# Where one rounding stands in ScalarE's queue, and which engines mask the scores of chunks 4 to 7

## The chip, the core and the metric

The kernel runs on one core of a Trainium2 chip. The core has a matrix engine (TensorE, PE in the profile), a vector engine (VectorE, DVE), a scalar engine (ScalarE, ACT), a general engine (GpSimd, POOL) and a queue that here issues the transfers (SyncE, SP). They run side by side and wait for each other through semaphores. The metric is device time in microseconds (us) of one execution.

## The reference

A gated linear attention (a recurrence over 768 steps for each of 4 batches and 8 heads), followed by two matrix products with a SiLU between them. Inputs: q, k, v, alpha of shape (4, 8, 768, 48), w_in (384, 2048), w_out (2048, 384).

```python
for t in range(S):                                  # S = 768
    state = alpha[:, :, t, :, None] * state + np.einsum('bhd,bhe->bhde', k[:, :, t], v[:, :, t])
    y[:, :, t] = np.einsum('bhd,bhde->bhe', q[:, :, t], state)
x = y.transpose(0, 2, 1, 3).reshape(3072, 384)      # tokens x (heads * 48)
h = x @ w_in
out = (h * (1.0 / (1.0 + np.exp(-h)))) @ w_out
```

## The kernel before

The sequence is cut into chunks of 128 tokens; with 4 batches there are 24 chunks, numbered n = 0 to 23. Each chunk goes through four stages: `products` (transposes of alpha, k, q; running products of alpha by a scan), `scores` (q times k, masked so that a token sees only earlier ones), `values` (masked scores times v, plus the state from before), `states` (the new state). At each step of the main loop the four stages work on neighbouring chunks, and after each stage `fill` puts in other work: at first conversions of weights, later the feed-forward products.

The weights come as 64-bit numbers and are made 32-bit numbers piece by piece. Here is that generator; `rounding` is ScalarE's part, the three `dve` lines are VectorE's. The rounding of the next piece is issued ahead, as soon as the present one's VectorE part is in the queue.

```python
def weights(which):
    # ... pieces: 12 of w_in (128 x 512) for which == 0, 16 of w_out (128 x 384) for which == 1
    def rounding(bits):
        n = bits.shape[1]
        up = upp.tile([128, 512], I32, name="up")[:, 0:n]
        tc.keep_in_program_order(
            act.activation(up, bits.bitcast(U32)[:, :, 0], AF.Copy, scale=2.0**-29))
        return up

    ahead = []
    for i, (dst, src) in enumerate(pieces):
        # ...
        bits = coming.pop(0)                       # a piece that was fetched before
        up = ahead.pop() if ahead else rounding(bits)
        hi, w = bits[:, :, 1], dst.bitcast(I32)
        tc.keep_in_program_order(                  # L623, L624, L625 in the profile
            dve.tensor_scalar(w, hi, 3, 0x3FFFFFFF, ALU.logical_shift_left, ALU.bitwise_and))
        dve.scalar_tensor_tensor(w, hi, -(1 << 30), w, ALU.bitwise_and, ALU.bitwise_or)
        dve.tensor_tensor(w, w, up, ALU.add)
        if i + 1 < len(pieces):
            ahead.append(rounding(coming[0]))      # L609
        fetch()                                    # issues the load of a later piece
        yield
```

The scores. GB is 4, NA is 8: chunks 0 to 3 are masked by a ScalarE copy out of PSUM and a GpSimd select, chunks 4 and up by a VectorE product with a mask.

```python
def scores(n):
    # ... ps: two PSUM banks of the three in ps_attn(); matmuls of kp and qp into them (L757)
    g = c["g"] = work.tile([128, 2, NP, C], F32, name="g")
    for u in range(2):
        if n < GB:
            act.copy(g[:, u], ps[u])                                        # L763
            gps.affine_select(g[:, u], g[:, u], pattern=[[0, NP], [1, C]], compare_op=ALU.is_ge,
                              fill=0.0, base=0, channel_multiplier=-1)      # L764
            continue
        m = mask[:, :, None, :] if n >= NA else mask[:, 0:1, None, :]
        dve.tensor_tensor(g[:, u].rearrange("p (o j) c -> p o j c", o=2),   # L768
                          ps[u].rearrange("p (o j) c -> p o j c", o=2),
                          m.to_broadcast([128, 2, NP // 2, C]), ALU.mult)
    if ci < NCH - 1:
        ps_k = ps_attn()
        # ... transposes of kp into ps_k (L774)
        act.copy(c["kn"], ps_k)                                             # L776
    # ... for ci > 0: the old state is scaled by ScalarE (L780)
```

Other lines that the profile names. L694: transposes of alpha (an), k (kn) and q (qn) on PE; L696: ScalarE's copy of the transposed alpha (al); L699, L728: the two scans on VectorE; L709, L733: its products that make kp and qp; L800: the matmuls of `values`; L805: ScalarE's copy of their result (xt); L815 and L821, L823: the states; L858: the matmuls with w_in (two blocks of 128 columns at a time, six matmuls); L861: SiLU; L971: a VectorE sum of two SiLU results; L980: matmuls with w_out; L498: the loads of weight pieces.

The main loop and the placing of the conversions (SLOTS is 4; marks[0] is 10; a "slot" is one stage's place in a step). `convert(0, k)` runs the generator of w_in until k pieces are done.

```python
def fill(step, slot):
    at = step * SLOTS + slot
    if at < marks[0]:
        if step >= 1:
            convert(0, (at - SLOTS) * 3 // (marks[0] - SLOTS) + 1)
        return
    # ... feed-forward pieces with the conversions that they need

for step in range(STEPS):
    # ...
    stages = [[(scores, 1)], [(products, 0)], [(values, 1)], [(states, 1)]]
    if step == 1:
        stages = stages[1::-1] + stages[2:]        # products of chunk 1, then scores of chunk 0
    # ... for each slot: its stages, then fill(step, slot)
```

So in step 1 the first slot is `products` of chunk 1, followed by the first conversion, and the second slot is `scores` of chunk 0.

Of the kernel before, what the change touches and what calls it, by code (L numbers as in the profile page):

```python
# [355 lines left out]
def quotients(  # L356
# [32 lines left out]
    GB = 4  # L389
# [28 lines left out]
    def ps_attn(n=C):  # L418
        return ps_a.tile([128, 512], F32, name="ps_a").rearrange("p (j c) -> p j c", c=n)
# [18 lines left out]
    NA = 2 * GB  # L438
# [53 lines left out]
    def fetch():  # L492

        if wide and sources:
            src = sources.pop(0)
            n = src.shape[1]
            bits = raw.tile([128, 512, 2], I32, name="bits")[:, 0:n, :]
            nc.sync.dma_start(bits.rearrange("p n w -> p (n w)"), src.bitcast(I32))  # L498
            coming.append(bits)
# [30 lines left out]
    mask = consts.tile([128, 2, C], F32, name="mask")  # L530
    gps.memset(mask, 1.0)
    for odd in range(2):
        for e in range(2):
            m = mask[CH * e : CH * e + CH, odd, :]
# [59 lines left out]
    def weights(which):  # L594

        pieces = [
            (w_in[:, t, c : c + 512], moe_w_in[t * 128 : t * 128 + 128, c : c + 512])  # L600
            for t, c in pieces_in
        ] if which == 0 else [
            (w_out[:, f, :], moe_w_out[f * 128 : f * 128 + 128, :]) for f in range(NFT)]
# [10 lines that stand above are left out]
            if not wide:  # L614
                act.dma_start(dst, src)
                yield
                continue
            assert which == 0 or conv_done[0] == n_conv[0]
            bits = coming.pop(0)
            up = ahead.pop() if ahead else rounding(bits)  # L620
            hi, w = bits[:, :, 1], dst.bitcast(I32)
            tc.keep_in_program_order(
                dve.tensor_scalar(w, hi, 3, 0x3FFFFFFF, ALU.logical_shift_left, ALU.bitwise_and))  # L623
# [4 lines that stand above are left out]
            fetch()  # L628
            yield
# [114 lines left out]
    def scores(n):  # L744
        c = ctxs[n]
        ci, b = c["ci"], c["b"]
        ps = c.pop("blank") if n >= NA else [ps_attn() for _ in range(2)]

        for j in (0, 2, 1, 3):
            for e in range(2 if n >= NA else 1):
                for u in range(2):
                    r = slice(64 * u, 64 * u + D)
                    at = slice(CH * e, CH * e + CH) if n >= NA else slice(0, C)
                    t = slice(CH * (e ^ j // 2) if n >= NA else 0, C)
                    pe.matmul(ps[u][at, j, t], lhsT=c["kp"][r, j, at], rhs=c["qp"][r, j, t],  # L757
                              start=True, stop=True)
        g = c["g"] = work.tile([128, 2, NP, C], F32, name="g")
        for u in range(2):  # L760
            if n < GB:

                act.copy(g[:, u], ps[u])  # L763
                gps.affine_select(g[:, u], g[:, u], pattern=[[0, NP], [1, C]], compare_op=ALU.is_ge,  # L764
                                  fill=0.0, base=0, channel_multiplier=-1)
                continue
            m = mask[:, :, None, :] if n >= NA else mask[:, 0:1, None, :]
            dve.tensor_tensor(g[:, u].rearrange("p (o j) c -> p o j c", o=2),  # L768
                              ps[u].rearrange("p (o j) c -> p o j c", o=2),
                              m.to_broadcast([128, 2, NP // 2, C]), ALU.mult)  # L770
        if ci < NCH - 1:
            ps_k = ps_attn()
            for j in range(NP):
                pe.transpose(ps_k[:, j, :], c["kp"][:, j, :], ident)  # L774
            c["kn"] = work.tile([128, NP, C], F32, name="kn")
            act.copy(c["kn"], ps_k)  # L776
        if ci > 0:
            s = st[b].rearrange("p j u e -> p j (u e)")
            for j in range(NP):
                act.mul(s[:, j], s[:, j], least[:, n, j : j + 1])  # L780
# [192 lines left out]
    def leave(grp, h):  # L973
# [70 lines left out]
        yield  # L1044

    conv = [weights(0), weights(1)]
    n_conv = (NKT * (DF // 512), NFT)
    conv_done = [0, 0]

    def convert(which, upto):  # L1050
        while conv_done[which] < min(upto, n_conv[which]):
            next(conv[which], None)
            conv_done[which] += 1
# [38 lines left out]
    def go_on():  # L1092

        nonlocal done
        next(pieces[done][0], None)
        done += 1
# [4 lines left out]
    SLOTS = 4  # L1101
# [14 lines left out]
    def fill(step, slot):  # L1116

        at = step * SLOTS + slot
        if at < marks[0]:
            if step >= 1:  # L1120
                convert(0, (at - SLOTS) * 3 // (marks[0] - SLOTS) + 1)
            return
        i = next(i for i, m in enumerate(marks[1:]) if at < m)
        a, b = [work_at[n] for n in ([0] + phases)[i : i + 2]]
        due = a + (b - a) * (at - marks[i] + 1) / (marks[i + 1] - marks[i])
        if at % 2 == 0 and step > 3 * GB + 2:
            next(audits, None)
        while work_at[done + 1] <= due and pieces[done][2] <= bridged:
            convert(0, 3 * (done // 2) + 6)
            convert(1, 3 * (done - 6) // 2)  # L1130
            go_on()

    for step in range(STEPS):
        if step == 1:
            load(NIN)
        stages = [[(scores, 1)], [(products, 0)], [(values, 1)], [(states, 1)]]
        if step == 1:

            stages = stages[1::-1] + stages[2:]
        elif step >= NA:  # L1140
            stages = [[(scores, 1)], [(products, 0)], [(values, 1), (states, 1)], [(quotient, 0), (blank, 0)]]
        for slot, group in enumerate(stages):
            for stage, lag in group:
                n = step - lag
                if not 0 <= n < NT:
                    continue
                stage(n)
                if stage is values:
                    bridged = n + 1
                if stage is states and n + 1 + NIN < NA:  # L1150
                    load(n + 1 + NIN)
                if stage is quotient and n + 1 < NT:
                    load(n + 1)
                if stage is states and n + NV < NT:
                    load_v(n + NV)
            fill(step, slot)
            if step * SLOTS + slot >= NA * SLOTS - 1 and conv_done[1] == NFT and not late:
                settle()
# [85 lines left out]
```

## Time and profile before

| what | value |
|---|---|
| time, median of 3 runs | 563.04 us (562.8 to 563.6) |
| span of the profiled run | 561.6 us |
| PE busy | 543.9 us (97%) |
| PE weight loads busy | 492.6 us (88%) |
| DVE busy | 453.0 us (81%) |
| ACT busy | 205.3 us (37%) |
| POOL busy | 15.1 us (3%) |
| mean granted PE clock | 0.994 |
| DMA moved | 63.81 MB, mean 114 GB/s |

How to read the profile's lines. A group or timeline row has the engine, the line of the kernel, the operation, `out<-in` by the program's names, sizes in partitions x elements, and the number of instructions merged into it (x2). In a timeline the first number is the start in us from the start of the span, the second the duration; brackets at the end hold the idle time of that engine just before, and which instruction or transfer ended it. A row of the table of stretches has the stretch in us, its length, then for each engine the busy time with the number of instructions, and last the granted PE clock, the mean busy share of the 16 DMA engines (over 1 when packets overlap) and GB/s. A row of waits has who waited for whom: us in total, how many times, the longest. Each fp32 matmul shows up as two records, so that six matmuls are x12.

### The profile page before, as it was taken

The numbers are of one execution on the slowest core, as the hardware profiler recorded it, in microseconds if no ns is written. First come the engines' busy times: TensorE is split into PE (matmuls) and PEld (weight loads), VectorE is DVE, ScalarE is ACT, GpSimd is POOL, SyncE is SP. The second block draws the span as 40 slices with busy tenths as digits, with TensorE's granted clock in tenths as the row PEclk, the third lists the DMA queues.
The fourth block names the chain that finished last, engine by engine and source line by source line (L and its number), as shares of the span: only waits on it lengthen the run. The fifth ranks groups of instructions, "written<-read, shape, count | busy, mean of one in ns | idle before, by whom it ended". The sixth has DMA issues, their size and how long they took to land.

```text
span 561.6 us, 12420 instructions
## 1 busy us (share of the span) xinstructions
PE 543.9 (97%) x5074; PEld 492.6 (88%) x5074; DVE 453.0 (81%) x829; ACT 205.3 (37%) x406; POOL 15.1 (3%) x36
## 2 busy tenths in 40 slices
PE   5899999999999999999999999999999999999996
PEld 3688887998999999899989999999998999899995
DVE  5797899966999799986998897899895875857731
ACT  2566543213233342443433443434443342332100
POOL 4211000100000000000000000000000000000000
PEclk9899999999999999999999999999999999999998
DMA  9989971143443333333425544435522123334200
GB/s 206 230 241 223 234 183 34 43 126 100 100 107 89 73 97 87 101 87 85 131 70 160 142 108 134 130 81 153 136 69 81 53 85 118 99 94 125 71 30 26
DMA packets 94417, 63.81 MB, mean 114 GB/s; under 512 B 55312, under 2 KB 86032, under 8 KB 94352
## 3 DMA queue, kind: packets, MB, share of 16 engines
q1 hardware_dynamic: 94352, 62.94, 43.3%
q8 instruction: 41, 0.67, 0.5%
q14 instruction: 24, 0.20, 0.1%
HBM read 58.20 MB, written 4.72 MB: 112 GB/s over the span
## 4 chain that ended last, share of the span: by engine, by line
PE 75%; DVE 14%; DMA 5%; SPq 2%; issue 2%; ACT 1%; POOL 0%; DVEq 0%; ACTq 0%
PE ps_o L980 33%; PE ps_m L882 18%; PE ps_m L858 11%; PE ps_a L800 6%; DMA bits<-in_moe_w_out_dram 3%; PE ps_a L757 3%; DVE seen L663 2%; PE ps_a L774 1%; DVE g L896 1%; DMA bits<-in_moe_w_in_dram 1%; DVE u L699 1%; PE ps_a L815 1%; DVE w_out L625 1%; DVE p L728 1%; SPq L456 1%
## 5 line engine op out<-in xcount | busy, mean ns | idle before, releaser
L980 PE MATMUL ps_o<-w_out,g 128*128 128x192 f32 x768 | 133.6, 328 | 1.1 <-DVE o L994 1.1
L980 PEld LDWEIGHTS ps_o<-w_out,g 128*128 128x128 f32 x768 | 125.5, 190 | 3.9 <-DVE o L994 1.5
L980 PE MATMUL ps_o<-wt,g 128*128 128x192 f32 x576 | 100.0, 327 | 0.0
L980 PEld LDWEIGHTS ps_o<-wt,g 128*128 128x128 f32 x576 | 95.1, 190 | 1.5
L858 PE MATMUL ps_m<-xt,w_in 128*128 128x256 f32 x384 | 88.5, 382 | 1.0 <-ACT xt L805 1.0
L858 PEld LDWEIGHTS ps_m<-xt,w_in 128*128 128x128 f32 x384 | 71.0, 190 | 11.0 <-ACT xt L805 1.4
L882 PE MATMUL ps_m<-xc,w_in 128*128 128x256 f32 x288 | 70.1, 379 | 0.0
L882 PEld LDWEIGHTS ps_m<-xc,w_in 128*128 128x128 f32 x288 | 54.0, 190 | 6.4 <-DVE g L896 0.2
L663 DVE TENSOR_REDUCE seen<-bits 128x1 f32<-128x384 int32 (+2 forms) x65 | 42.4, 689 | 16.8 <-DMA bits<-in_moe_w_out_dram 16.5
L893 ACT ACTIVATE g<-g 128x1024 f32<-128x1024 f32 x32 | 33.1, 1055 | 57.5 <-DVE g L896 57.5
L985 DVE TENSOR_TENSOR g<-g 128x512 f32<-128x512 f32 x72 | 48.5, 686 | 5.6 <-PE ps_o L980 5.6
L882 PE MATMUL ps_m<-xc,wx 128*128 128x256 f32 x192 | 50.1, 383 | 0.0
L888 ACT COPY g<-ps_m 128x512 f32<-128x512 f32 x64 | 36.8, 587 | 36.1 <-PE ps_m L882 36.0
L780 ACT ACTIVATE st<-st,least 128x96 f32<-128x96 f32 x80 | 24.1, 364 | 58.4 <-DVE least L702 58.4
L882 PEld LDWEIGHTS ps_m<-xc,wx 128*128 128x128 f32 x192 | 35.0, 190 | 4.2 <-issue 0.4
L896 DVE TENSOR_TENSOR g<-ps_m,g 128x512 f32<-128x512 f32 x56 | 37.4, 683 | 0.8 <-PE ps_m L882 0.5
L699 DVE TENSOR_TENSOR_SCAN u<-al,one 128x516 f32<-128x516 f32 x24 | 29.1, 1212 | 10.4 <-ACT al L696 10.3
L728 DVE TENSOR_TENSOR_SCAN p<-al,inv 128x516 f32<-128x516 f32 x24 | 29.4, 1226 | 5.2 <-PE ps_a L800 4.9
L861 ACT ACTIVATE g<-ps_m 128x512 f32<-128x512 f32 x32 | 19.0, 595 | 39.2 <-PE ps_m L858 39.0
L800 PE MATMUL ps_a<-g,vn 128*32 128x128 f32 x768 | 28.0, 282 | 3.9 <-POOL g L764 3.9
L800 PEld LDWEIGHTS ps_a<-g,vn 128*32 128x32 f32 x768 | 20.3, 112 | 11.2 <-issue 5.5
L768 DVE TENSOR_TENSOR g<-ps_a,mask 128x512 f32<-128x512 f32 x40 | 25.7, 685 | 4.0 <-PE ps_a L757 3.7
(125 smaller groups left out, 620.7 us busy)
## 6 DMA issues: line engine op xcount, KB each, us to landing
bits<-in_moe_w_in_dram SPq DMA_DIRECT2D x24, 512.0 KB, 4.7
bits<-in_moe_w_out_dram SPq DMA_DIRECT2D x32, 384.0 KB, 3.4
at<-in_alpha_dram SPq DMA_DIRECT2D x64, 96.0 KB, 2.4
kt<-in_k_dram SPq DMA_DIRECT2D x64, 96.0 KB, 2.6
qt<-in_q_dram SPq DMA_DIRECT2D x64, 96.0 KB, 2.5
bits<-in_alpha_dram SPq DMA_DIRECT2D x9, 512.0 KB, 3.8
out_dram<-o SPq DMA_DIRECT2D x48, 96.0 KB, 1.9
an<-in_alpha_dram SPq DMA_DIRECT2D x8, 192.0 KB, 5.1
```

The costliest lines, as they stand in the source:

```text
L663: dve.tensor_reduce(seen[kind][which][:, i : i + 1], x, axis=AX, op=op, apply_absolute_value=True))
L699: dve.tensor_tensor_scan(u[:, end - 1 :: -1], sg[:, end:0:-1], one[:, end:0:-1], 0.0, ALU.mult, ALU.add)
L728: dve.tensor_tensor_scan(p[:, 0:end], sg[:, 0:end], iv[:, 0:end], 0.0, ALU.mult, ALU.add)
L768: dve.tensor_tensor(g[:, u].rearrange("p (o j) c -> p o j c", o=2), ps[u].rearrange("p (o j) c -> p o j c", o=2), m.to_broadcast([128, 2, ...
L800: pe.matmul(py[32 * at : 32 * at + 32, t, :], lhsT=w, rhs=x, start=(i < 4), stop=(i >= len(todo) - 4), skip_group_check=True)
L858: pe.matmul(ps[:, e, :], lhsT=w_in[:, t, (f + e) * 128 : (f + e + 1) * 128], rhs=xt[:, t, :], start=(t == 0), stop=(t == NKT - 1))
L882: pe.matmul(ps[:, e], lhsT=block_w(w)[:, 2 * pair + e], rhs=block_x(grp, x), start=(first and e == 0), stop=(e == 1), skip_group_check=True)
L888: act.copy(to, ps)
L893: act.activation(x, x, AF.Silu)
L896: dve.tensor_tensor(to, a, b, op)
L980: pe.matmul(ps, lhsT=x, rhs=w[:, i], start=(first and i == 0), stop=(i == HF - 1), skip_group_check=True)
L985: dve.tensor_tensor(cells(grp, h, pair, *to), cells(grp, h, pair, *x), cells(grp, h, pair, *y), ALU.subtract)
```

## The change

Two things are changed. The first moves one ScalarE instruction. The generator now stops once, in its first piece, right after the first rounding; the first slot of step 1 runs it only up to there, and the second slot, after the scores of chunk 0, runs the rest of the first piece. The rounding of the second piece, which is issued at the end of the first piece, so comes behind ScalarE's copies of the first scores instead of ahead of them. It is meant to keep those copies from waiting for a weight load. The second widens the path by ScalarE and GpSimd from chunks 0 to 3 to chunks 0 to 7; it is meant to take the mask products of chunks 4 to 7 off VectorE.

```diff
@@ weights
             bits = coming.pop(0)
             up = ahead.pop() if ahead else rounding(bits)
+            if which == i == 0:
+                yield
             hi, w = bits[:, :, 1], dst.bitcast(I32)
@@ scores
         for u in range(2):
-            if n < GB:
+            if n < NA:
 
                 act.copy(g[:, u], ps[u])
                 gps.affine_select(g[:, u], g[:, u], pattern=[[0, NP], [1, C]], compare_op=ALU.is_ge,
                                   fill=0.0, base=0, channel_multiplier=-1)
                 continue
-            m = mask[:, :, None, :] if n >= NA else mask[:, 0:1, None, :]
+            m = mask[:, :, None, :]
@@ fill
         if at < marks[0]:
-            if step >= 1:
+            if at == SLOTS:
+                next(conv[0])
+            elif step >= 1:
                 convert(0, (at - SLOTS) * 3 // (marks[0] - SLOTS) + 1)
             return
```

## Prediction

> **What bounds the kernel now.** I read the busy times first, then busy time by stretch of the span, then the waits of TensorE, then the timeline of the first 30 us, and last the chain of waits around 70 to 102 us. TensorE (PE) is busy 543.9 of 561.6 us and the chain that ended last is 75% PE, so only a PE that is idle, or runs below its clock, can give time back. The table of stretches tells where that is. Its columns are: stretch, length, busy us of PE, of PE's weight loads, of VectorE (DVE), ScalarE (ACT) and GpSimd (POOL), the granted PE clock, the busy share of the DMA engines, GB/s.
>
> ```profile
> 10.00:14.00 4.00, 2.28 (x24) 1.75 (x24) 3.83 (x7) 0.96 (x2) 0.00 (x0) 1.00 1.07 331
> 14.00:25.00 11.00, 8.74 (x158) 6.84 (x158) 7.89 (x13) 6.39 (x14) 3.16 (x4) 0.84 1.22 256
> ...
> 25.00:102.00 77.00, 75.39 (x694) 63.01 (x695) 68.38 (x129) 38.00 (x79) 3.58 (x4) 1.00 0.72 180
> 102.00:214.00 112.00, 112.00 (x1301) 102.69 (x1300) 94.76 (x180) 36.78 (x85) 2.17 (x3) 1.00 0.36 90
> 214.00:300.00 86.00, 85.26 (x847) 77.65 (x850) 77.44 (x139) 35.18 (x69) 0.00 (x0) 1.00 0.38 102
> ```
>
> From 10 to 25 us PE is idle for 1.72 + 2.26 = 4.0 us. From 25 to 102 us it is idle for only 1.6 us, from 102 to 214 us never. The change acts in the first two places; the rest of the span can only be shifted by it.
>
> The idle time of 10 to 25 us is one wait, seen in the timeline (start us, duration us, engine, line, operation; in brackets the idle time before it and who ended it):
>
> ```profile
> 11.39 0.69 ACT L609 ACTIVATE up<-bits 128x512 int32<-128x512 uint32 x1 [1.92 <-DMA bits<-in_moe_w_in_dram]
> 13.73 0.67 ACT L609 ACTIVATE up<-bits 128x512 int32<-128x512 uint32 x1 [1.65 <-DMA bits<-in_moe_w_in_dram]
> 14.30 1.05 ACT L763 COPY g<-ps_a 128x512 f32<-128x512 f32 x2
> 15.24 0.60 ACT L776 COPY kn<-ps_a 128x512 f32<-128x512 f32 x1
> ...
> 14.94 1.94 POOL L764 TENSOR_SCALAR_AFFINE_SELECT g<-g 128x512 f32<-128x512 f32 x2 [7.91 <-ACT g L763]
> ...
> 15.89 0.64 PE L800 MATMUL ps_a<-g,vn 128*32 128x128 f32 x4 [3.62 <-POOL g L764]
> ...
> 16.93 1.71 PE L800 MATMUL ps_a<-g,vn 128*32 128x128 f32 x26 [0.24 <-POOL g L764]
> ```
>
> The first chunk's scores are done at 11.69 (they start at 10.53 and take 1.16), but ACT sits in front of them in the rounding of the second weight piece, whose data lands only at 13.71 (issued at 7.61, 6.1 us to landing). Behind it come the copy of the scores, GpSimd's masking, and PE's values.
>
> [...] ACT waits 1.65 us for the load with finished scores behind it. [...] the select takes 0.63 us at best and 1.08 at worst, and the third step of a weight conversion (L625), 0.69 us alone, took 0.90 beside the selects at 15.48. [...]
>
> ```profile
> 12.13:15.54 3.41, 0.15 (x2) 0.00 (x0) 3.10 (x7) 1.81 (x4) 0.60 (x1) 1.00 1.11 338
> 15.54:18.96 3.42, 2.82 (x56) 2.44 (x58) 3.25 (x5) 0.36 (x2) 1.34 (x2) 0.50 1.26 244
> ```
>
> PE worked 0.15 us of the first window and was given half clock in the second.
>
> **Part A: the second rounding behind the copies.** I listed both kernels' instructions engine by engine. PE's and SyncE's orders are unchanged; on ACT only the second rounding moves, behind the two score copies and the kn copy, and the masks of part B are added.
>
> 1. The copies can start when the scores are ready and the first rounding is out, at 12.0 instead of 14.30: 2.3 us earlier. kn then ends at about 13.6.
> 2. GpSimd follows 0.64 us behind (14.94 − 14.30): 12.65. Its two selects end at about 14.6 at the latest, against 16.88. PE's values restart there instead of at 16.93: 2.3 us.
> 3. The second rounding now stands at 13.7, as before, since its data is what it waits for. VectorE wants it at about 18.0 (the L625 of the second piece), so nothing is lost.
> 4. What follows on PE (scores of the second chunk, transposes of the third) moves up by as much as its inputs allow. The transposes need loads that do not move, since SyncE issues them in the same order behind other loads and the DMA engines are full (share 1.07 and 1.22):
>
> ```profile
> 22.20 0.66 PE L694 MATMUL ps_o<-ident,kn 128*128 128x128 f32 x4
> 23.57 0.66 PE L694 MATMUL ps_o<-ident,qn 128*128 128x128 f32 x4
> ...
> kn<-in_k_dram SPq DMA_DIRECT2D x1, 192.0 KB, 8.2
> ...
> qn<-in_q_dram SPq DMA_DIRECT2D x1, 192.0 KB, 6.1
> ```
>
> The last number is us from issue to landing, asked for the third chunk's loads alone: k is issued at 11.86 and lands at 20.06, q at 15.00 and lands at 21.1. PE used them at 22.20 and 23.57, so they allow 2.1 and 2.5 us. Alpha (issued 11.37, 7.5 us to land, used at 21.16) allows 2.3. The smallest sets the shift: 2.1 us. The first large matmul (L858) comes at about 23.1 instead of 25.18.
> 5. Does it last? From 25.18 on the chain is PE with short links through ACT. The conversions of w_in are nearly a second bound: the third pair of L858 starts at 32.54 and the piece that it needs ends at 32.92. But VectorE's run up to there begins with a scan at 23.17 that waited 2.47 us for an ACT copy of those same transposes, so it moves up with them. The weight data allows it: the sixth piece, issued at 18.34, landed at 25.15 and was converted at 30.95. I keep 2.1.
>
> **Part B: masks of chunks 4 to 7.** Taken off VectorE: 8 products of 686 ns, 5.2 us as pairs of 1.29. Added: 8 copies on ACT at 0.53 (4.3 us, ACT is busy 50.6 of the 114 us from 14 to 128) and 8 selects on GpSimd (5 to 8 us, GpSimd is free). What counts is where PE waits for VectorE. That is only in 86 to 102 us:
>
> ```profile
> PE ps_a L815 <- DVE kp L709: 0.5, 1, 0.5
> PE ps_m L858 <- ACT xt L805: 0.4, 1, 0.4
> PE ps_a L774 <- DVE st L821: 0.2, 1, 0.2
> ```
>
> So at most 1.1 us are there to win, and the mask that stands before it is chunk 5's:
>
> ```profile
> 82.87 1.29 DVE L768 TENSOR_TENSOR g<-ps_a,mask 128x512 f32<-128x512 f32 x2
> 85.63 0.68 DVE L971 TENSOR_TENSOR g<-g 128x512 f32<-128x512 f32 x1
> 86.23 1.23 DVE L699 TENSOR_TENSOR_SCAN u<-al,one 128x516 f32<-128x516 f32 x1
> ...
> 84.87 0.60 ACT L861 ACTIVATE g<-ps_m 128x512 f32<-128x512 f32 x1 [0.96 <-PE ps_m L858]
> ```
>
> Without the mask VectorE would reach L971 at 84.34, but L971 sums what that Silu writes, up to 85.47, and the scan needs ACT's al copy, up to 85.94. So VectorE gains 0.2 us there, not 1.29. On ACT the new copies push kn from 83.33 to 84.4, the Silu to 85.0 and the al copy by some 0.1. I count 0.1 us gained. Chunk 4's mask (65.86) stands before a VectorE wait of 0.89 us for another Silu, and chunks 6 and 7 (104.12 and 117.64) where PE never waits: 0.
>
> **Sum.** 563.04 − 2.1 − 0.1 = 560.8 us.
>
> **Rivals.** *The loads bind.* DMA is full to 25 us and its share is 0.89 from 25 to 70; the last two w_in pieces landed (issue and time to landing) at 43.98 and 45.25 and were converted at 44.80 and 46.69. If these do not move up, half the shift is lost by 48 us: 561.9. For it speaks the share; against it that a piece is fetched when its buffer is free, which moves up too, and that no wait for DMA is on PE after 10.5 us. *PE keeps its full clock.* The idle gap of 3.6 us shrinks to some 2, so the half-clock window may vanish; PE's 2.8 busy us in it would take some 1.4 less. The loads of point 4 hold most of that back, but VectorE would come out ahead of PE and the conversions be early: 560.2. *ACT becomes the bound.* Copies in front of the Silu and al copies of chunks 4 and 5 hold up score banks and the scan, with GpSimd's select ending as late as the values want it (both near 85.9 for chunk 5): 0.3 to 0.6 us back, 561.3. *VectorE's relief counts in full:* 1.1 us more, 559.7; the Silu in front of it speaks against.
>
> **Range and chances.** 559.7 to 562.3 holds the rivals singly and leaves a little for two at once. 2% is 11.3 us, more than PE's idle time over the parts that the change touches (5.6 us), so faster by that has 0.01. Slower by 2% would need a new wait of 11 us that no order shows: 0.01.
>
> **What would show it.** Right: score copies at 12.0, values restarting before 14.7, first L858 near 23.1, the second rounding still at 13.7, and an offset of about 2 us at every later landmark (first L980 near 100.1). The three waits of 86 to 102 us still there with about 1 us. Wrong: L858 later than 24, waits of PE for loads in 18 to 22 us beyond 0.5, a shift that shrinks between 25 and 50 us (loads), or one that grows by 0.5 us or more between 70 and 102 us (the masks mattered after all).

## The result, and the profile after

| | before | changed |
|---|---|---|
| time, median (lowest to highest), 4 runs each | 562.99 us (562.8 to 563.6) | 561.19 us (560.85 to 561.29) |
| ratio, 95% interval | | 0.9965 [0.9948, 0.9982] |
| span of the profiled run | 561.6 us | 559.1 us |

In the changed kernel all lines from the generator of the weights on stand two lower (L858 is L860, L694 is L696, L763 and L764 are L765 and L766); L609 is the same. The versions of the experiments shift the numbers by their own edits; the operations and names tell what is what.

The table of stretches of the changed kernel, in the columns of before:

```profile
10.00:14.00 4.00, 2.29 (x27) 1.77 (x28) 3.83 (x7) 2.53 (x5) 1.51 (x2) 1.00 1.08 333
14.00:25.00 11.00, 9.78 (x162) 7.79 (x160) 9.49 (x16) 5.50 (x12) 2.07 (x3) 0.84 1.21 253
25.00:102.00 77.00, 75.57 (x699) 63.53 (x699) 65.01 (x123) 40.60 (x84) 6.83 (x10) 1.00 0.74 180
```

PE's idle time from 10 to 25 us fell from 4.0 to 1.71 + 1.22 = 2.9 us, and from 25 to 102 us from 1.61 to 1.43. So about 1.2 us came from where the change acts. The first half of the reason is in the timeline of 11 to 17 us:

```profile
11.27 0.68 ACT L609 ACTIVATE up<-bits 128x512 int32<-128x512 uint32 x1 [2.39 <-DMA bits<-in_moe_w_in_dram]
11.85 1.05 ACT L765 COPY g<-ps_a 128x512 f32<-128x512 f32 x2
12.49 1.91 POOL L766 TENSOR_SCALAR_AFFINE_SELECT g<-g 128x512 f32<-128x512 f32 x2 [5.48 <-ACT g L765]
...
13.59 0.69 ACT L609 ACTIVATE up<-bits 128x512 int32<-128x512 uint32 x1 [0.20 <-DMA bits<-in_moe_w_in_dram]
...
14.45 1.71 PE L802 MATMUL ps_a<-g,vn 128*32 128x128 f32 x26
...
16.43 0.48 ACT L807 COPY xt<-ps_a 128x384 f32<-128x384 f32 x1 [2.15 <-PE ps_a L802]
```

The score copies follow the first rounding at once, 2.45 us earlier than before (14.30), GpSimd follows 0.64 behind, the second rounding keeps its place, and the first chunk's result (xt) is copied at 16.43 instead of 18.91. Up to here the change brings 2.5 us. PE's next transposes and the first w_in matmul:

```profile
20.24 0.66 PE L696 MATMUL ps_o<-ident,kn 128*128 128x128 f32 x4
...
22.47 0.66 PE L696 MATMUL ps_o<-ident,qn 128*128 128x128 f32 x4 [0.68 <-DMA qn<-in_q_dram]
...
24.08 1.13 PE L860 MATMUL ps_m<-xt,w_in 128*128 128x256 f32 x4 [0.26 <-ACT xt L807]
```

The last of these lines in the kernel before:

```profile
25.18 1.13 PE L858 MATMUL ps_m<-xt,w_in 128*128 128x256 f32 x4 [0.26 <-ACT xt L805]
```

The k transposes are 2.0 us earlier than before (22.20), the q transposes only 1.1 (23.57), because PE now waits for the load of q. From here the lead is 1.10 us: xt of the second chunk 23.55 against 24.65, first w_in matmul 24.08 against 25.18. It is 1.28 at xt of the fourth chunk (54.42 against 55.70) and 1.29 still at the last chunk's xt (445.81 against 447.10). The masks changed nothing in 86 to 102 us, where the changed kernel's waits of PE are (who waited for whom, us in total, times, longest):

```profile
PE ps_a L817 <- DVE kp L711: 0.5, 1, 0.5
PE ps_a L776 <- DVE st L823: 0.4, 1, 0.4
PE ps_m L860 <- ACT xt L807: 0.3, 1, 0.3
```

Before, the waits for xt and st were 0.43 and 0.23 us, now they are 0.30 and 0.35; the sum of the three is 1.16 us, as it was.

**Why q is late.** SyncE issues it as early as before (14.86 against 15.00), but it lands at 22.43 instead of 21.06. Three lines of the DMA view of the changed kernel, for 18.8 to 19.0 us, for 21 to 22 us, and for the issues from 14.8 to 17.2 us:

```profile
q8 instruction: 1, 0.02, 45.7%
...
DMA packets 145, 0.40 MB, mean 400 GB/s; under 512 B 49, under 2 KB 49, under 8 KB 145
...
qn<-in_q_dram SPq DMA_DIRECT2D x1, 192.0 KB, 7.6
```

And two of the kernel before, for 20.0 to 20.2 us and for 21 to 22 us:

```profile
q8 instruction: 1, 0.02, 45.8%
...
DMA packets 106, 0.38 MB, mean 377 GB/s; under 512 B 14, under 2 KB 14, under 8 KB 106
```

q8 is a queue that the profile calls `instruction`: 41 packets and 0.67 MB in either kernel, so 16 KB each. That it brings the program's own instructions is read from that name alone. A packet starts at 20.11 us in the kernel before and at 18.89 in the changed one, and takes 1.46 us. q is made of rows of 192 bytes. In the kernel before only 14 packets under 512 bytes are left from 21 to 22 us, none of them of 192 bytes; in the changed kernel there are 49, of which 33 have 192 bytes. Those are the tail of q: of the 16 completions that the trace has for this load, 15 were in by 20.85 us, the last at 22.43, as if one of the 16 DMA engines alone had been held up. The experiments test whether the packet is the cause.

**The rest of the profiled difference** arises at one place late in the span. Before:

```profile
482.36 1.01 DVE L663 TENSOR_REDUCE seen<-bits 128x1 f32<-128x384 int32 x2 [0.43 <-DMA bits<-in_moe_w_out_dram]
...
483.69 2.54 PE L980 MATMUL ps_o<-w_out,g 128*128 128x192 f32 x14 [1.07 <-DVE o L994]
```

After:

```profile
479.88 1.02 DVE L665 TENSOR_REDUCE seen<-bits 128x1 f32<-128x384 int32 x2
...
481.22 2.87 PE L982 MATMUL ps_o<-w_out,g 128*128 128x192 f32 x16
```

There VectorE reads the weights through for a side task (L663). In the profiled run before, it waited for a load, and PE waited 1.07 us behind it; in the profiled run after, PE did not. Just ahead of this place PE's lead is still 1.28 us, behind it 2.47 (483.69 against 481.22). The other profiled runs have 0 to 0.7 us at this place, with the change (0.66 in e3) and without it (0.43 in e11). So this microsecond is an accident of two executions and no effect of the change.

### The profile page after: what moved, and what is told of

It reads as the page before. It is cut to its first block, busy times and chain, and to the rows that moved or that the text cites. A ratio compares the mean times of both kernels' runs of the same rounds, so it can differ in the third digit from the quotient of the medians.

```text
span 559.1 us, 12435 instructions
## 1 busy us (share of the span) xinstructions
PE 543.4 (97%) x5074; PEld 492.6 (88%) x5074; DVE 448.1 (80%) x821; ACT 208.9 (37%) x414; POOL 20.8 (4%) x44
## 4 chain that ended last, share of the span: by engine, by line
PE 79%; DVE 12%; DMA 3%; ACT 2%; SPq 1%; issue 1%; POOL 0%; DVEq 0%; ACTq 0%
PE ps_o L982 35%; PE ps_m L884 21%; PE ps_m L860 11%; PE ps_a L802 6%; PE ps_a L759 3%; PE ps_a L776 2%; DMA qn<-in_q_dram 1%; DVE g L898 1%; DMA bits<-in_moe_w_in_dram 1%; DVE u L701 1%; PE ps_a L817 1%; DVE p L730 1%; DVE seen L665 1%; SPq L456 1%; DVE w_out L626 1%
## 5 line engine op out<-in xcount | busy, mean ns | idle before, releaser
L860 PE MATMUL ps_m<-xt,w_in 128*128 128x256 f32 x384 | 88.3, 382 | 0.8 <-ACT xt L807 0.8
L860 PEld LDWEIGHTS ps_m<-xt,w_in 128*128 128x128 f32 x384 | 71.1, 190 | 10.6 <-ACT xt L807 1.2
L890 ACT COPY part<-ps_m 128x512 f32<-128x512 f32 x32 | 18.6, 582 | 21.8 <-PE ps_m L884 17.6
```

Of the source, the lines that this page charges most:

```text
L860: pe.matmul(ps[:, e, :], lhsT=w_in[:, t, (f + e) * 128 : (f + e + 1) * 128], rhs=xt[:, t, :], start=(t == 0), stop=(t == NKT - 1))
L890: act.copy(to, ps)
```

## The experiments

The kernel before ran beside e1 to e10. Its median was 563.91 us in the first group of runs (e1 to e4), 563.08 in the second (e5 to e7) and 563.98 in the third (e8 to e10), so ratios are compared and not times.

### Each part alone, and the changed kernel again

e1 keeps the moved rounding and undoes the masks; e2 has the masks alone:

```diff
 e1 (from the changed kernel)            e2 (from the kernel before)
-            if n < NA:                  -            if n < GB:
+            if n < GB:                  +            if n < NA:
```

e1: 

> Only the second rounding is moved; the masks stay as before. Theory (instruction fetch): the rounding gives the whole early gain, first score copies near 11.9, values from 13.9, but a 16 KB packet of the instruction queue starts near 18.9 us and holds one DMA engine for 1.5 us, so that the third chunk's q lands near 22.4 instead of 21.1, and the first L858 comes near 24.1: a shift of 1.1 us there, 1.1 to 1.3 us at 300 us. Time 1.1 to 1.9 us under the kernel before. Rival (q's late landing was chance): q lands at 21.0 to 21.5, the first L858 comes before 23.4, shift 1.9 us or more. Rival (the masks give part of it): time under 0.8 us better than before.

e2: 

> Only the masks of chunks 4 to 7 go to ScalarE and GpSimd; the rounding stays. Theory: no more than 0.3 us either way, since VectorE's sum L971 and its scan wait for ScalarE in front of the only place where TensorE waits for VectorE (86 to 102 us); the first L858 near 25.2, the instruction packet near 20.1 and q at 21.0 to 21.2. Rival (VectorE's relief counts): 0.6 to 1.2 us faster, with the waits of TensorE in 86 to 102 us gone. Rival (masks cost): 0.3 to 0.6 us slower.

e3: 

> The changed kernel once more, for what repeats. If the instruction packet follows the program's progress, it starts at 18.6 to 19.2 again and q lands 22 or later, the first L858 at 23.9 to 24.3. If it was chance, q lands near 21. The wait of 1.1 us for VectorE near 483 us, which the profile of the kernel before has and the changed kernel's had not: if it is chance, it can be here or not, and the difference of the two spans (2.5 us) overstates the gain; expected time 1.3 to 2.0 us under the kernel before.

e10: 

> The changed kernel once more, as the measure for the run beside it on the same chip. All theories: ratio 0.995 to 0.997 to the kernel before; instruction packet at 18.9 us, q landing at 22.4, first w_in matmul at 24.1.

| run | ratio, 95% interval | packet starts | q lands | first w_in matmul |
|---|---|---|---|---|
| e1, rounding only | 0.9961 [0.9949, 0.9973] | 18.86 | 22.39 | 24.05 |
| e2, masks only | 0.9996 [0.9985, 1.0008] | 20.18 | 21.18 | 27.66 |
| e3, changed kernel | 0.9952 [0.9935, 0.9970] | 18.96 | 22.43 | 24.09 |
| e10, changed kernel | 0.9956 [0.9939, 0.9972] | 18.95 | 22.47 | 24.25 |

One of the fourteen executions of e1 took 808 us, at a mean granted clock of 0.66, and is left out of its ratio. The gain is that of the rounding; the masks by themselves give nothing that can be measured. PE's waits of e2 from 84 to 104 us, in the kernel's old line numbers, are those of the changed kernel, though the lead of the rounding is missing:

```profile
PE ps_a L815 <- DVE kp L709: 0.5, 1, 0.5
PE ps_a L774 <- DVE st L821: 0.4, 1, 0.4
PE ps_m L858 <- ACT xt L805: 0.3, 1, 0.3
```

q is late in all three runs with the moved rounding and not in e2. The late start of w_in in e2 goes with the clock: its second chunk's scores took 2.09 us, against 1.36 in the kernel before; more of this below.

### q ahead of the fourth weight piece

e4 is the changed kernel with q of the third chunk issued ahead of the fourth weight piece:

```diff
-    for i in range(4):        # weight pieces fetched before the loop
+    for i in range(3):
...
     for step in range(STEPS):
         if step == 1:
             load(NIN)         # alpha, k, q, v of the third chunk
+            fetch()
```

> The changed kernel with the fourth weight piece fetched after the third chunk's alpha, k and q instead of ahead of them. Theory (q's landing holds TensorE at 21.8 to 22.5 us): q is issued about 1.3 us earlier and lands near 20 to 21 even with the packet, the wait of 0.7 us goes, and the first L858 comes near 23.0 to 23.4: 0.7 to 1.1 us faster than the changed kernel, if the fourth piece (landing near 22, converted at 25.3) still comes in time. Rival (the shift is capped by something else, such as ScalarE's copies or the score banks): first L858 stays at 23.8 to 24.1, time within 0.3 us of the changed kernel.

Ratio 0.9948 [0.9928, 0.9968], no different from e3. SyncE issues q no earlier than in e3 (14.98 us against 14.91), but the weight piece now comes behind it, and q landed at 19.68. The timeline of e4:

```profile
20.18 0.60 PE L696 MATMUL ps_o<-ident,qn 128*128 128x128 f32 x4
...
23.39 1.78 PE L860 MATMUL ps_m<-xt,w_in 128*128 128x256 f32 x7 [0.83 <-ACT xt L807]
...
46.31 1.67 POOL L766 TENSOR_SCALAR_AFFINE_SELECT g<-g 128x512 f32<-128x512 f32 x2 [13.83 <-ACT g L765]
46.49 0.99 DVE L627 CUSTOM_DVE_ANT_0 w_in<-w_in,up 128x1024 uint16<-128x1024 uint16 x1
...
47.54 0.70 PE L860 MATMUL ps_m<-xt,w_in 128*128 128x256 f32 x2 [0.52 <-DVE w_in L627]
```

Without the wait for q the first w_in matmul comes 0.7 us earlier than in e3. So the wait does hold the start. But at 47 us PE waits 0.52 us for VectorE's conversion of the last w_in piece, a wait that e3 does not have, and from xt of the fourth chunk (54.52) on e4 is where e3 is. VectorE is the second bound behind q: from 20.6 to 47.5 us its only pause over 0.14 us is one of 0.37 at 31.2, for the load of a weight piece. A part of the wait is a collision: the last step of the conversion (L627) runs beside a GpSimd select and takes 0.99 us instead of 0.69. In the five profiles that have this wait (e4 to e8) that step took 0.90 to 1.12 us, in the nine others 0.69. How much of the 0.52 us is the collision, and how much VectorE's other work and its load, was not tested apart.

e9 takes one instruction out of that stretch. The first sum of SiLU results (0.6 us of VectorE at 40 us) is put behind the last conversion:

```diff
 (from e4)
+        if at == 16:                   # in fill
+            side_by_side(0, 0, 0)      # left out at its old place
```

> The version with q issued before the fourth weight piece, and VectorE's first sum of two SiLU results (0.6 us at 40.4 us, used at 100) put behind the last w_in conversion. Theory (the lead of 0.7 us that q first brings is lost at 47 us because VectorE, without a pause from 20.6 to 47.5 us, delivers the last w_in piece 0.52 us late): the last conversion ends 0.6 us earlier, TensorE's wait of 0.52 us at 47.0 is gone, and every later landmark is 0.5 us earlier than in that version: xt of the fourth chunk at 54.0 instead of 54.5, time 0.5 us below the changed kernel, ratio to the kernel before about 0.994. Rival (another wait takes its place, for the weight data or for ScalarE): the landmarks from 54 us on are those of the changed kernel, ratio 0.995.

The timeline of e9:

```profile
21.41 0.66 PE L696 MATMUL ps_o<-ident,qn 128*128 128x128 f32 x4 [1.03 <-DMA qn<-in_q_dram]
...
46.52 0.69 DVE L627 CUSTOM_DVE_ANT_0 w_in<-w_in,up 128x1024 uint16<-128x1024 uint16 x1
47.13 1.12 DVE L975 TENSOR_TENSOR g<-g 128x512 f32<-128x512 f32 x1
```

The last conversion ends before PE wants it, and the wait at 47 us is gone. Not only the sum is away, though: the last step of the conversion (46.52) began just ahead of the select (46.62) and took 0.69 us. xt of the fourth chunk is at 54.25 instead of 54.52, and that lead stays to the end (445.62 against 445.89). But q, issued as early as in e4, landed at 21.37 in this execution, so that the first w_in matmul came at 23.71 instead of 23.39, and about half of the lead was lost there. The ratio is 0.9954 [0.9936, 0.9971] against 0.9956 for e10 beside it: a few tenths of a microsecond are seen in the profile and none in the times. No version here is measurably faster than the changed kernel.

e7 tried another relief, GpSimd for the four sums of the first group:

```diff
 (from e4)
-        dve.tensor_tensor(x, x, cells(grp, h, pair, 1, 1), ALU.add)
+        (gps if grp == 0 else dve).tensor_tensor(x, x, cells(grp, h, pair, 1, 1), ALU.add)
```

> Experiment 4's kernel with the four sums L973 of the first group of chunks on GpSimd instead of VectorE (0.68 us each at about 40, 55, 68 and 84 us). Theory (VectorE is the bound from 20 to 47.5 us): the last w_in conversion ends 0.4 to 0.7 us earlier, the wait of 0.52 us at 47 us shrinks below 0.2, and the scan at 85 us starts at most 0.2 earlier since it waits for ScalarE; time 0.3 to 0.7 us under experiment 4. Rival (loads are the bound there): the wait at 47 us stays at 0.4 to 0.6. Rival (GpSimd's two-input sum slows VectorE beside it): time as experiment 4 or 0.3 us slower.

It made the kernel slower than e4: 0.9987 [0.9980, 0.9994]. The timeline of e7 shows two losses:

```profile
21.00 1.09 PE L696 MATMUL ps_o<-ident,qn 128*128 128x128 f32 x4 [1.57 <-DMA qn<-in_q_dram]
...
39.30 1.51 POOL L973 TENSOR_TENSOR g<-g 128x512 f32<-128x512 f32 x1 [5.84 <-ACT g L863]
...
39.81 2.09 DVE L730 TENSOR_TENSOR_SCAN p<-al,inv 128x516 f32<-128x516 f32 x1
...
69.66 1.27 POOL L973 TENSOR_TENSOR g<-g 128x512 f32<-128x512 f32 x1 [0.73 <-ACT g L863]
...
70.08 1.93 DVE L701 TENSOR_TENSOR_SCAN u<-al,one 128x516 f32<-128x516 f32 x1 [2.62 <-ACT al L698]
...
89.37 0.54 PE L817 MATMUL ps_a<-vn,kn 128*32 128x48 f32 x30 [1.11 <-DVE kp L711]
```

First, q is late (20.96, with the packet at 17.45), PE waits 1.57 us, and in the 3.41 us after that wait the granted clock is 0.50. The stretch of e7 from 21.07 us:

```profile
21.07:24.48 3.41, 3.41 (x66) 2.88 (x66) 3.24 (x6) 1.14 (x3) 0.00 (x0) 0.50 1.20 298
```

The first w_in matmul comes at 24.56, 1.17 us after e4's. Second, GpSimd's sum takes 1.27 us at 69.66 (VectorE's 0.69), and the scan that starts beside it takes 1.93 instead of 1.23; the lag behind e4 grows from 1.18 us at xt of the fourth chunk to 2.23 at that of the sixth. The wait for the last w_in piece was still there, 0.52 us at 48.2: the first of the sums, at 39.30, slowed the scan beside it to 2.09 us, so that VectorE lost 0.86 us there where the moved sum had saved 0.67, and the last step of the conversion again stood beside a select (0.98 us).

### The packet without the rounding

e8 is the kernel before with eight more transposes, where PE only waits:

```diff
-            for j in range(NP):                          # NP is 4
-                pe.transpose(ps_k[:, j, :], c["kp"][:, j, :], ident)
+            for j in range(12 if n == 0 else NP):
+                pe.transpose(ps_k[:, j % NP, :], c["kp"][:, j % NP, :], ident)
```

> The kernel before with eight more transposes of the first chunk's kp, behind the four that it has, in the stretch from 12.3 to 15.9 us where TensorE only waits. Their results are written twice over and change nothing. TensorE passes 16 more pairs of load and multiply by that place, nothing else comes earlier. Theory (the 16 KB packet of the instruction queue follows how many instructions TensorE has taken, and delays the load of q when it comes before that load is through): the packet, at 20.1 us in the kernel before, comes at about 18.5 to 19.2, and q lands at about 22.4 instead of 21.1, with nothing of the rounding changed. q is used at 23.57, so the time stays within 0.2%. Rival (q lands late because the moved rounding lets other loads be issued earlier and go in between): q lands at 21.0 to 21.2 as before. A second question is the clock: with the eight transposes TensorE works in the window that was nearly empty, so the half clock from 15.5 to 19 us may fall away; then the first w_in matmuls come up to 0.5 us earlier, held by q.

The packet came at 18.58 instead of 20.11 us and q landed at 22.03 instead of 21.06, with the rounding where it was before and the score copies at 14.36. The timeline of e8:

```profile
12.94 1.53 PE L774 MATMUL ps_a<-ident,kp 128*128 128x128 f32 x12
...
24.20 1.13 PE L858 MATMUL ps_m<-xt,w_in 128*128 128x256 f32 x4 [0.27 <-ACT xt L805]
```

So the packet comes earlier when PE has taken more instructions, and q comes late when the packet comes early, without the change. This speaks against the rival that other loads got between. In all fourteen profiles PE had begun 112 to 134 matmul records when the packet started (121 in the kernel before, 128 in the changed one), though that was anywhere from 17.4 to 23.5 us. The ratio is 0.9991 [0.9979, 1.0002]. PE had its full clock from 12.75 us on in this run, already before the extra transposes: the twelve transposes at 12.94 took 1.53 us, where e11's four at half clock took 1.11. It reached w_in a microsecond earlier than in the profile of before, but there was a wait of 0.52 us for the last w_in piece at 47.8, and xt of the fourth chunk came at 55.34, only 0.36 ahead.

All profiled runs with q at its old place in the order of loads agree: packet at 19.94 to 20.29 us, q at 20.99 to 21.32 (before, e2, e11, e12); packet at 18.48 to 18.96, q at 22.00 to 22.47 (changed kernel, e1, e3, e5, e8, e10). In these six late ones the last of the sixteen completions of q came 1.1 to 1.6 us behind the fifteenth, in the four early ones at most 0.13 us. With q issued ahead of the fourth piece it is less regular: packet 17.45 and q 20.96 (e7), 18.85 and 21.37 (e9), but 18.64 and 19.68 (e4); with the packet out of the way at 23.45, q at 19.80 (e6). In e7 and e9 one completion is late again, in e4 and e6 none. In e4 the packet may have met a DMA engine that was through with q. The packets' records do not name their engine, so that this stays open, as does how to keep the packet out of the way.

### A warm start

e5 and e6 give PE eight transposes of the identity at the very start, before its first inputs arrive, in the kernel before and in e4:

```diff
+    warm = out_bank(0, 512)
+    for _ in range(8):
+        pe.transpose(warm[:, 0:128], ident, ident)
```

e5: 

> The kernel before, with eight transposes of the identity on TensorE while it waits for the first alpha (1.5 to 4.1 us); nothing reads them. Theory (part of the gain is the clock): the kernel before runs, in some executions, at half clock up to 25.7 us, as the profile of the masks-only kernel showed, which puts the first L858 at 27.7 instead of 25.2 and makes its times spread from 562.5 to 565.7; TensorE that works from 1.5 us is given full clock earlier, so the median falls to 562.4 to 563.3 and the highest stays under 564.4. Rival (the spread is not the clock): median within 0.3 us of the kernel before, highest above 565.

e6: 

> Experiment 4's kernel (the rounding moved, the masks moved, the fourth piece fetched after the third chunk's loads) with the same eight transposes at the start. The first values come at 13.8 to 14.0 instead of 14.5, and the first L858 at 22.6 to 23.1. Theory (VectorE's conversions of w_in are the next bound up to 47.5 us, where TensorE waited 0.52 us for the last one): the lead is lost by 48 us, time within 0.3 us of experiment 4. Rival (the clock still costs there): 0.5 us or more faster than experiment 4.

Both were slower: e5 1.0033 [1.0023, 1.0043], e6 1.0046 [1.0032, 1.0060]. They are no clean test of the clock, because the program was put together in another order. The timeline of e5:

```profile
9.37 1.23 DVE L703 TENSOR_TENSOR_SCAN u<-al,one 128x516 f32<-128x516 f32 x1 [1.36 <-ACT al L700]
...
10.52 1.21 DVE L732 TENSOR_TENSOR_SCAN p<-al,inv 128x516 f32<-128x516 f32 x1
...
13.03 1.16 PE L761 MATMUL ps_a<-p,kp 48*128 48x128 f32 x16 [2.09 <-DVE p L737]
```

VectorE runs the second chunk's scan (L703) ahead of the first chunk's p scan (L732, at 8.17 in the kernel before), and the first scores start at 13.03 instead of 10.53. Nor did PE stay at its clock: 0.50 was granted from 14.52 to 24.76 us. In e6 a k transpose was also put in front of the rest of the first values, PE waited 1.28 us there for its load, and the first w_in matmul came at 27.22 us instead of the 22.6 to 23.1 that were expected.

### The kernel before, twice more

> The kernel before, profiled once more, for two readings. Packet theory: the instruction packet at 20.1 to 20.2 us and q landing at 21.0 to 21.2, whatever the clock does. Clock theory (the times of the kernel before spread over 3 us, those of the changed kernel over 1, because TensorE sometimes begins at half clock, and then its wait from 12 to 16 us puts off the full clock): where the first chunk's scores take about 2.1 us instead of 1.16, the first w_in matmul comes after 27 us and the time is above 564.9 us; where they take 1.16, it comes at 25.2 and the time is 562.3 to 564.2 us. Rival: a slow beginning is made up by 26 us, so that the first w_in matmul is at 25.2 us in both cases.

> The same kernel and the same two readings as in the run beside it; a second execution, since the beginning of the clock can't be chosen.

e11 took 565.29 us, e12 564.00. The timeline of e11:

```profile
11.08 2.08 PE L757 MATMUL ps_a<-p,kp 48*128 48x128 f32 x16
...
19.52 2.09 PE L757 MATMUL ps_a<-p,kp 48*128 48x128 f32 x16
```

And of e3, the changed kernel with as slow a beginning:

```profile
10.92 2.08 PE L759 MATMUL ps_a<-p,kp 48*128 48x128 f32 x16
...
17.20 1.47 PE L759 MATMUL ps_a<-p,kp 48*128 48x128 f32 x16
```

The sixteen records of a chunk's scores are a gauge of the clock: 1.16 us at full clock for the first chunk (at 10.53 in the kernel before) and 1.36 to 1.47 for the second, 2.08 or 2.09 at half (2.09 at 19.39 in e12, where the clock column has 0.50). (The clock column of the stretches reads 1.00 ahead of the first record of the clock, as from 8.64 to 12.05 us in e11, where the scores took 2.08, so it can't be used there.) In e11 the first two chunks' scores both ran at half, full clock came at 25.71, and w_in began at 27.75. In e3 the second chunk's already ran at full clock, which came at 16.66, and w_in began at 24.09. e12 was in between: first scores 1.24 us, then half clock from 14.55 to 21.38, twice 3.41 us, and w_in at 26.21. Its time of 564.0 is in the range that was expected, its landmark is not (25.2): also a run that begins at full clock can be at half for 6.83 us instead of 3.41.

| | first w_in matmul, us | time of these runs, us |
|---|---|---|
| old place of the rounding: before, e12, e2, e11 | 25.18, 26.21, 27.66, 27.75 | 563.47, 564.00, 565.31, 565.29 |
| new place: changed kernel, e1, e3, e10 | 24.08, 24.05, 24.09, 24.25 | 560.85, 561.40, 561.90, 562.38 |

The rival, that a slow beginning is made up, falls. With the old place the start of w_in spreads over 2.6 us, with the new one over 0.2, and the times of the kernel before spread over 3 us (562.52 to 565.66 in the first group), those of the changed kernel over 1 within a group. That the emptier stretch from 12 to 16 us (PE busy for 2.16 of the 3.42 us from 12.05 in e11, for 3.08 of the 3.41 from 13.25 in e3) is what holds the half clock on is the reading that fits these eight runs, but the cause is not shown. e8, which puts work there, does not settle it: its full clock began ahead of the extra transposes, and its times still reach up to 565.28.

## Why the prediction was right

The time of 560.8 us was near (561.19), and the route to it was half right; that the time came so near is in part luck, as the last point tells.

- **A1 to A3, right.** Copies at 11.85 (12.0 foreseen), GpSimd at 12.49 (12.65), values back at 14.45 (14.6 at the latest), second rounding at 13.59 (13.7).
- **A4, the mis-sized term.** It said that the transposes need loads "that do not move", so that k with its 2.1 us would set the shift. k landed almost as before (19.90 against 20.06), but q moved back by 1.4 us. PE waited 0.68 us for it, more than the 0.5 set as a limit, and the first w_in matmul came at 24.08, past the limit of 24 and far from 23.1. The term is 1.1 us instead of 2.1 in the two profiles. The order of the loads was indeed the same; overlooked was the instruction packet, which moved up with PE's work, from 20.11 to 18.89 us.
- **A5, right.** The lead lasted: 1.10 at 24 us, 1.28 from 54 us to the end of the attention. The rival of the loads in its own form, half the shift lost by 48 us, did not come. e4 shows how near it was: with more lead, the wait for the last w_in conversion takes 0.5 us back.
- **B, right.** 0.1 us was foreseen; e2 gives 0.9996, or 0.2 us with an interval of about 0.6 to either side, and the three waits are 1.16 us together, as before.
- **What made up for A4.** 2.1 us were asked of the rounding, 1.3 are in the steady part of the two profiles, and the medians differ by 1.8 in the first comparison and by about 2 in e3 and e10. The difference fits the clock, though that is not shown: in other executions the kernels with the old place start w_in 1.0 to 2.6 us later than the first profile of before does, while those with the new place stay within 0.2 us. The rival *PE keeps its full clock* had the right subject. It did not happen in the form described. PE was busy for 1.72 us of the 3.42 from 10.91, where the kernel before had 0.15 from 12.13, and half clock was granted in the next 3.41 all the same:

```profile
10.91:14.33 3.42, 1.72 (x22) 1.24 (x20) 3.25 (x7) 2.81 (x5) 1.84 (x2) 1.00 1.06 336
14.33:17.74 3.41, 3.31 (x65) 3.05 (x66) 3.07 (x6) 1.30 (x4) 0.07 (x1) 0.50 1.19 270
```

Half clock also followed on such stretches with 1.49 (e5), 1.63 (e12) and 1.84 us (e7) of work: they need not be as empty as the one in the prediction (0.15 us). What varies besides is how long half clock lasts: 3.41 us in the kernel before, 6.83 in e12, 10.24 in e5.

## What to carry to other kernels

In the kernel before, ScalarE waited 1.65 us for a weight load with finished scores behind it. An instruction that waits for a transfer should not stand in an engine's queue ahead of one whose data is ready: move it behind. Here its own consumer lost nothing, since the rounding still began when its data came (13.59 against 13.73). But look for the next bound before counting the whole gap, and include traffic that the program does not issue itself: here the instruction packet moved up by 1.22 us with PE's work, and a load that PE was about to need landed 1.37 us later. And when two profiles differ by 2.5 us, go landmark by landmark, since here 1.2 of it was an accident at a single place, and one profile of each kernel did not show how far the start spreads from one execution to the next.

## What the runs showed of the hardware

- **Where a 16 KB instruction packet started earlier, a load landed 0.9 to 1.4 us later than in the kernel before.** The packet takes 1.46 us at 18.89 us in the changed kernel. With q at its old place in the order of loads, q landed at 20.99 to 21.32 where the packet started after 19.9 (four profiles) and at 22.00 to 22.47 where it started before 19.0 (six), and in these six a single completion of its sixteen was late.
- **Half clock can outlast busy stretches.** In the profiles of the kernel before and the changed one, the granted clock changes at times that are 3.41 us apart or a multiple of it (before: half from 15.54, full from 18.96, half again from 558.26). In e2 PE was busy for 3.24 of the 3.42 us from 8.61 and for all of the 3.42 from 18.85, and full clock came only at 25.68. That the clock was still at half is seen from the work itself, the second chunk's scores (2.09 us) and, after 22.27, the k transposes (1.12 us, 0.66 at full clock); the 1.00 in the rows stands ahead of the first record of the clock. So such a busy stretch was not enough here:

```profile
8.61:12.03 3.42, 3.24 (x19) 2.52 (x20) 3.28 (x6) 1.26 (x2) 0.00 (x0) 1.00 1.14 272
...
18.85:22.27 3.42, 3.42 (x44) 3.00 (x36) 1.54 (x3) 2.29 (x6) 0.08 (x1) 1.00 1.21 285
...
19.37 2.09 PE L757 MATMUL ps_a<-p,kp 48*128 48x128 f32 x16
...
23.85 1.12 PE L694 MATMUL ps_o<-ident,kn 128*128 128x128 f32 x4
```

Stretches filled with transposes and scores came out both ways: in e8 full clock followed at once on 9.33 to 12.75 us, in e3 it did not on 9.83 to 13.25 (it came at 16.66), with 3.42 us of work in both. What decides is open.
- **VectorE's scan takes longer beside a two-input sum on GpSimd.** In e7 the scan began at 70.08 beside a GpSimd sum that ended at 70.93, and took 0.70 us more than its 1.23, with 0.85 us of overlap. At 39.81 it took 0.86 us more, with 1.00 of overlap. In both the loss was a little less than the overlap; its cause was not shown.
